# Value weights in quarters, half-depth value steps and another order in an attention and channel-mix kernel

## The chip, the cores and the metric

The kernel runs on one core of one Trainium2 chip. The metric is the device time of one execution in microseconds, lower is better.

## The reference

Eight batches of eight heads, 576 tokens, 64 dimensions each. Attention goes through 32 memory slots per head; its output, 512 wide, goes through a channel mix with squared relu and a sigmoid gate. All inputs are float32.

```python
a = softmax(phi, axis=2)                       # over the 576 tokens
k_m = einsum('bhsm,bhsd->bhmd', a, k)
v_m = einsum('bhsm,bhsd->bhmd', a, v)
attn = softmax(q @ k_m.T / 8)                  # over the 32 slots
x = (attn @ v_m)                               # 8 heads side by side: [8, 576, 512]
x_prev = x shifted by one token, zero first
xk = mu_k * x + (1 - mu_k) * x_prev
xr = mu_r * x + (1 - mu_r) * x_prev
k = relu(xk @ w_k)                             # 512 -> 1024
v = (k * k) @ w_v                              # 1024 -> 512
out = sigmoid(xr @ w_r) * v
```

## The kernel before, in words

Everything is issued in an order written out by hand: `PLAN` is a list of words, each names one step, and every engine gets its instructions in the order of the words. `BANKS` gives, one digit for each PSUM tile in the order in which tiles are asked for, which of the eight PSUM banks it takes. The order in which a step comes on one engine is therefore fixed; between engines semaphores decide.

The words: a number before the colon is a batch. `exp` exponentiates phi (ScalarE), `ko` makes the memory keys and the sums of the slots on TensorE, `v` the memory values (`kov` both), `zk` takes the reciprocals, `nk`/`ak` normalises keys on VectorE or ScalarE, `nv`/`av` the values, `tk`/`ta` transposes the keys and copies them out on VectorE or ScalarE, `q0`, `q1` transpose q on VectorE, `s` makes the scores and exponentiates them, `fe`, `fs`, `fo` (and `qe`, `qs`, `qo` in quarters) fold, sum and spread the denominators on VectorE, and `y0` to `y3` give the attention weights `atn` (L431). Batch 0 has its own way to the mixed input: `mk0`, `mk1`, `mr0`, `mr1` (L245 matmuls, then casts, L458) write the inputs of keys (k) and gates (r) for the first 320 and the last 256 tokens; each takes four PSUM banks. `busyNxM` issues N matmuls of zeros, M blocks of 128 columns wide (L215), which nothing reads.

From batch 1 on tokens go in chunks of 512 (the eighth 448), across batches. `x1:v` makes chunk 1's x in transposed form, ScalarE casting it (with `m` VectorE casts half), `d` subtracts the previous token, `k` and `r` scale the difference by mu and add it (scaled on VectorE with ending `d`, L562, on ScalarE with `e`, L560) into the rings `xkT` and `xrT`. Then follow

- `c1:3`: key matmuls for 128 of the 1024 features and a chunk's tokens (L617), relu on ScalarE (L621), square on VectorE (L629) or, with ending `s`, on ScalarE (L627). Chunk 0 is batch 0 and goes in halves, `a` of 320 and `b` of 256 tokens;
- `g:7`: the gate of a 128-token tile, four matmuls (L650) and a tanh (L653);
- `o:7`: the value of a tile, eight matmuls (L667), product with the gate on VectorE (L669), two stores. `o:1a` and `o:1b` are the halves of 256 columns.

There are 36 tiles for `g` and `o`. `p:` words are loads; almost all are issued on GpSimd's queue, in the order of the words, and cast float32 to bf16 on the way. `p:wk:4-8` is the half of wk for features 512 to 1023, `p:wv:0-2` the half of wv for output columns 0 to 255. Each buffer is loaded again only when its last reader is done.

Of the kernel before, what the change touches and what calls it, by code (L numbers as in the profile page):

```python
# [10 lines left out]
F32 = mybir.dt.float32  # L11
# [5 lines left out]


PLAN = [
# [24 lines left out]
]  # L44

LOADS = {None: ("phi", "k", "v", "q")}
PRE = "k:0a id:"
BANKS = (
    "01234567012367540123675403612754036127546203715462073154620731546207315462037416520374165724031567240315"
    "67203415672034162053472053416720534720516372401637254016354106732541067325410673254173254173065412730652"  # L50
    "73041652730416527304165274163052741630527416305276413052764130527641305276413"
)


NJ = 9
# [6 lines left out]
def kernel(  # L62
# [34 lines left out]
    psum = ctx.enter_context(tc.psum_pool(name="psum", bufs=1))  # L97
# [4 lines left out]
    def bank():  # L102
        return f"ps{next(banks)}"
# [16 lines left out]
    def load_phi(b, eng):  # L120
        ph = ld.tile([128, HH, NJ, M], F32, name="ph", tag=f"ph{b % 2}")
        eng.dma_start(out=ph.rearrange("p h j m -> p h (j m)"), in_=rows(phi[b]))
        loads[b] = ph

    def load_rows(dst, src):
        nc.gpsimd.dma_start(out=dst.rearrange("p h j d -> p h (j d)"), in_=rows(src))
# [25 lines left out]
    wv_sb = big.tile([128, NF, Dm], BF16, name="wv")  # L152
# [7 lines left out]
    def preload(word):  # L160

        what, _, part = word.partition(":")
        if what in weights:
            dst, src = weights[what]
            f0, f1 = (int(x) * 128 for x in part.split("-"))
            nc.gpsimd.dma_start(out=dst[:, :, f0:f1], in_=src[:, :, f0:f1])
        elif what == "id":
            make_identity(nc, identity)
        else:
            n = int(part[0])  # L170
            if what == "phi":
                load_phi(n, nc.gpsimd)
            else:
                dst = qs[n % 2].rearrange("p (h j) d -> p h j d", j=NJ) if what == "q" else kvs[:, KV[n % 2]["k1v".index(what)]]
                src = {"q": q, "k": k, "v": v}[what][n]
                if len(part) == 1:
                    load_rows(dst, src)
                elif part[1] in "ab":
# [20 lines left out]
    for g in range(4):  # L199
        r = slice(g * M, (g + 1) * M)  # L200
# [8 lines left out]
    sq = big.tile([128, NF, 2 * S], BF16, name="sq")  # L209
# [379 lines left out]
        return steps  # L589


    def store(o, t, cols):
        g = t * 128
        eng = nc.sync
        while g < (t + 1) * 128:
            b, r = divmod(g, S)
            p = g - t * 128
            j, p0 = divmod(r, QR)
            j = (j + 1) % NJ if b else j
            n = min(QR - p0, (t + 1) * 128 - g)  # L600
            dst = out[b].rearrange("(p j) d -> p j d", j=NJ)[p0:p0 + n, j, cols]
            eng.dma_start(out=dst, in_=o[p:p + n, cols])
            if t >= NTOK // 128 - 2:
                eng = nc.scalar
            g += n

    def keys(c):
        start = STARTS[c]
# [28 lines left out]
    gated, outs, homes, parts = {}, {}, {}, {}  # L637
    free = {"sg": list(range(SG)), "o": list(range(4))}

    def take(name, t):  # L640
        homes[name, t] = free[name].pop(0)
        return work.tile([128, Dm], F32, name=name, tag=f"{name}{homes[name, t]}")
# [10 lines left out]
            nc.scalar.activation(gated[t], pr, AF.Tanh, scale=0.5)  # L653
        return go

    def value(t, hs=((0, 1),), n=1):

        def go():
            if t not in outs:
                outs[t] = take("o", t)  # L660
            o = outs[t]
            p = t * 128 % (2 * S)
            for h0, h1 in hs:
                cols = slice(h0 * Dm // n, h1 * Dm // n)
                pv = psum.tile([128, Dm], F32, name="pv", tag=bank())
                for fi in range(NF):
                    nc.tensor.matmul(pv[:, cols], lhsT=sq[:, fi, p:p + 128],  # L667
                                     rhs=wv_sb[:, fi, cols], start=(fi == 0), stop=(fi == NF - 1))
                nc.vector.scalar_tensor_tensor(o[:, cols], in0=gated[t][:, cols], scalar=1.0, in1=pv[:, cols],  # L669
                                               op0=AL.add, op1=AL.mult)  # L670
                store(o, t, cols)
                parts[t] = parts.get(t, 0) + Dm * (h1 - h0) // n
            if parts[t] == Dm:
                for name in free:
                    free[name].append(homes[name, t])
        return go

    NT = NTOK // 128
    chunks = {f"x{c}": chunk_steps(c) for c in range(1, len(STARTS))}
    mixes = {f"c{c}": keys(c) for c in range(len(STARTS))}  # L680
    mixes["g"] = {str(t): gate(t) for t in range(NT)}
    mixes["o"] = {str(t): value(t) if t < NT - 1 else value(t, ((0, 1), (1, 2)), 2) for t in range(NT)}
    for t in range(4):
        for h in range(2):
            mixes["o"][f"{t}{'ab'[h]}"] = value(t, ((h, h + 1),), 2)

    attend = [attention(b) for b in range(B)]
    todo = []
    for n, word in enumerate(" ".join(PLAN).split()):
        who, _, name = word.partition(":")  # L690
# [40 lines left out]
```

## Time and profile before

| what | value |
|---|---|
| runs | 200.18, 202.08, 202.23 us, median 202.08 |
| profiled execution | 200.59 us, span 198.8 us |
| granted TensorE clock | 0.991 |
| busy: TensorE, VectorE, ScalarE, GpSimd | 189.0, 155.5, 149.7, 29.8 us |
| moved by the software queue of GpSimd | 20.91 MB |

Busy time of TensorE counts a matmul up to its modelled end, so that 95% doesn't say that no time can be saved; the places where it waits, and for what, tell more. Times of the trace count from the first instruction.

### The profile page before, as it was taken

The numbers are of one execution on the slowest core, as the hardware profiler recorded it, in microseconds if no ns is written. First come the engines' busy times: TensorE is split into PE (matmuls) and PEld (weight loads), VectorE is DVE, ScalarE is ACT, GpSimd is POOL, SyncE is SP. The second block draws the span as 40 slices with busy tenths as digits, with TensorE's granted clock in tenths as the row PEclk, the third lists the DMA queues.
The fourth block names the chain that finished last, engine by engine and source line by source line (L and its number), as shares of the span: only waits on it lengthen the run. The fifth ranks groups of instructions, "written<-read, shape, count | busy, mean of one in ns | idle before, by whom it ended". The sixth has DMA issues, their size and how long they took to land.

```text
span 198.8 us, 5486 instructions
## 1 busy us (share of the span) xinstructions
PE 189.0 (95%) x2194; PEld 97.4 (49%) x2214; DVE 155.5 (78%) x428; ACT 149.7 (75%) x307; POOL 29.8 (15%) x45
## 2 busy tenths in 40 slices
PE   8978799999999999999999999999999999999992
PEld 3535565784454544445347644444443445444451
DVE  6179589898879998999699999998999998122232
ACT  2245899748987999999998899997878698935210
POOL 7843323211050210003500000000000000000000
PEclk9979999999999999999999999999999999999999
DMA  6999999999999999994999903212142027004345
GB/s 160 183 206 268 206 208 199 267 224 276 250 224 279 232 302 218 266 299 64 207 208 248 227 2 83 53 31 53 44 108 63 1 47 167 0 3 106 81 97 139
DMA packets 24522, 31.30 MB, mean 157 GB/s; under 512 B 1960, under 2 KB 19632, under 8 KB 24496
## 3 DMA queue, kind: packets, MB, share of 16 engines
q0 software_dynamic: 17392, 20.91, 56.4%
q1 hardware_dynamic: 6336, 9.18, 17.9%
q10 hardware_dynamic: 768, 0.85, 1.4%
q8 instruction: 17, 0.28, 0.5%
q14 instruction: 9, 0.07, 0.1%
HBM read 38.28 MB, written 9.44 MB: 240 GB/s over the span
## 4 chain that ended last, share of the span: by engine, by line
PE 70%; DMA 13%; DVE 9%; ACT 3%; issue 1%; POOL 1%; POOLq 0%; DVEq 0%
PE pv L667 26%; PE pk L617 25%; PE pr L650 13%; DMA wr<-in_moe_w_r_dram 9%; DMA q<-in_q_dram 4%; PE kvps L279 3%; DVE o L669 1%; DVE diff L545 1%; DVE sq L629 1%; PE scps L371 1%; PE nops L245 1%; ACT x L536 1%; ACT sg L653 1%; DVE xrT L567 1%; DVE lz L422 1%
## 5 line engine op out<-in xcount | busy, mean ns | idle before, releaser
L617 PE MATMUL pk<-xkT,wk 128*128 128x512 bf16 (+4 forms) x344 | 67.3, 340 | 1.0 <-ACT xkT L458 0.3
L667 PE MATMUL pv<-wv,sq 128*128 128x512 bf16 (+1 forms) x324 | 65.3, 353 | 0.2
L621 ACT ACTIVATE rl<-pk 128x512 bf16<-128x512 f32 (+3 forms) x80 | 42.9, 555 | 6.8 <-PE pk L617 4.2
L617 PEld LDWEIGHTS <-wk 128*128 128x128 bf16 x352 | 32.9, 98 | 29.3 <-issue 1.5
L667 PEld LDWEIGHTS <-sq 128*128 128x128 bf16 x328 | 31.4, 98 | 29.5 <-issue 0.4
L650 PE MATMUL pr<-wr,xrT 128*128 128x512 bf16 x136 | 34.8, 380 | 0.6 <-DMA wr<-in_moe_w_r_dram 0.2
L669 DVE SCALAR_TENSOR_TENSOR o<-sg,pv 128x512 f32<-128x512 f32 (+1 forms) x41 | 24.4, 614 | 11.5 <-PE pv L667 11.4
L560 ACT ACTIVATE mu_d<-diff,mu 128x512 bf16<-128x512 bf16 (+1 forms) x40 | 26.2, 716 | 6.1 <-DVE diff L550 2.9
L653 ACT ACTIVATE sg<-pr 128x512 f32<-128x512 f32 x36 | 20.9, 601 | 9.4 <-PE pr L650 5.7
L629 DVE TENSOR_TENSOR sq<-rl 128x320 bf16<-128x320 bf16 (+5 forms) x63 | 17.6, 314 | 12.2 <-ACT rl L621 11.9
L627 ACT ACTIVATE sq<-rl 128x512 bf16<-128x512 bf16 (+5 forms) x41 | 21.7, 543 | 1.1
L650 PEld LDWEIGHTS <-xrT 128*128 128x128 bf16 x144 | 13.5, 98 | 16.5 <-issue 0.8
L536 ACT CAST x<-nops 128x512 bf16<-128x512 f32 (+3 forms) x34 | 16.0, 572 | 2.0 <-PE nops L245 2.0
L431 DVE TENSOR_TENSOR atn<-e,lz 128x320 bf16<-128x320 bf16 (+1 forms) x32 | 13.2, 442 | 0.2
L545 DVE TENSOR_TENSOR diff<-x 128x1024 bf16<-128x1024 bf16 (+1 forms) x15 | 10.5, 699 | 2.6 <-ACT x L536 2.6
L422 DVE STREAM_TRANSPOSE lz<-se 128x320 f32<-128x320 f32 (+3 forms) x22 | 12.3, 572 | 0.2
L376 ACT ACTIVATE e<-scps 128x288 bf16<-128x288 f32 x32 | 10.5, 421 | 2.4 <-PE scps L371 2.4
L265 ACT ACTIVATE em<-ph 128x1152 bf16<-128x1152 f32 (+1 forms) x9 | 9.3, 1053 | 3.5 <-DMA ph<-in_phi_dram 3.5
L356 DVE STREAM_TRANSPOSE qT<-q 128x576 uint32<-128x576 uint32 x16 | 11.9, 757 | 0.0
L215 PE MATMUL idle<-zeros 128*128 128x512 bf16 (+2 forms) x44 | 10.9, 414 | 1.0 <-DVE zeros L144 1.0
L413 DVE TENSOR_REDUCE se<-eT 128x18 f32<-128x576 bf16 (+3 forms) x16 | 11.1, 696 | 0.2
L279 PE MATMUL kvps<-kvs,em 64*32 64x64 bf16 (+2 forms) x864 | 10.0, 220 | 1.2 <-DMA kvs<-in_k_dram 1.2
(72 smaller groups left out, 148.1 us busy)
## 6 DMA issues: line engine op xcount, KB each, us to landing
out_dram<-o SPq DMA_DIRECT2D x61, 128.0 KB, 2.5
kvs<-in_v_dram POOLq DMA_DIRECT2D x8, 576.0 KB, 15.5
ph<-in_phi_dram POOLq DMA_DIRECT2D x7, 576.0 KB, 18.8
kvs<-in_k_dram POOLq DMA_DIRECT2D x7, 576.0 KB, 19.0
q<-in_q_dram POOLq DMA_DIRECT2D x6, 576.0 KB, 18.9
q<-in_q_dram POOLq DMA_DIRECT2D x4, 288.0 KB, 10.1
out_dram<-o SPq DMA_DIRECT2D x18, 64.0 KB, 5.6
wk<-in_moe_w_k_dram POOLq DMA_DIRECT2D x2, 512.0 KB, 14.3
```

Of the source, the lines that this page charges most:

```text
L279: nc.tensor.matmul(kvps[c][g * M:(g + 1) * M], lhsT=em[ROWS[c], j, g, :], rhs=kvs[ROWS[c], at, g, j, :], start=j == 0, stop=j == NJ - 1, s ...
L422: nc.vector.transpose(st["lz"].rearrange("p c (b t h) -> p (c b) h t", t=PB, h=2)[:, b0:b0 + n], st["se"][:, b0:b0 + n].unsqueeze(3).to_br ...
L536: (nc.vector.tensor_copy if both and i % 2 else nc.scalar.copy)(x[:, i, c0:c1], pss[i])
L560: nc.scalar.activation(t[:, i, :n], ds[c][:, pr + i, :n], AF.Copy, scale=mu1[:, o:o + 1])
L617: nc.tensor.matmul(pk[:, p0 - lo:p1 - lo], lhsT=wk_sb[:, di, fi * 128:(fi + 1) * 128], rhs=xk_T[:, di, p0 % RING:p0 % RING + p1 - p0], sta ...
L621: nc.scalar.activation(rl, pk, AF.Relu, scale=HALF_ROOT)
L627: nc.scalar.activation(sq[:, fi, p:p + p1 - p0], rl[:, part], AF.Square)
L629: nc.vector.tensor_mul(sq[:, fi, p:p + p1 - p0], rl[:, part], rl[:, part])
L650: nc.tensor.matmul(pr, lhsT=xr_T[:, di, c0:c0 + 128], rhs=wr_sb[:, di, :], start=(di == 0), stop=(di == ND - 1))
L653: nc.scalar.activation(gated[t], pr, AF.Tanh, scale=0.5)
L667: nc.tensor.matmul(pv[:, cols], lhsT=sq[:, fi, p:p + 128], rhs=wv_sb[:, fi, cols], start=(fi == 0), stop=(fi == NF - 1))
L669: nc.vector.scalar_tensor_tensor(o[:, cols], in0=gated[t][:, cols], scalar=1.0, in1=pv[:, cols], op0=AL.add, op1=AL.mult)
```

## The change

- wv comes in four loads: columns 0 to 255 and 256 to 511, each for features 0 to 511 (`l`) and 512 to 1023 (`u`).
- A value half of tiles 0 to 3 can be made in two steps of four matmuls, which share a PSUM bank: `e` and `f` for columns 0 to 255, `c` and `d` for 256 to 511. The bank stays taken from the first step of a tile until its last such step is evicted. In tile 1 all four steps share one bank, and only the first matmul of the first step carries the start flag.
- In the order: phi of batch 1 is loaded ahead of wk's first half; batch 0's four mixes stand together, and five of chunk 0's keys, from features 512 to 1023, stand ahead of batch 1's `ko`; all sixteen keys of chunk 0 stand ahead of the first gate; the other steps move by a few places, some change their engine.
- At the end tile 33 is made in halves, the second one last, and tile 35 whole. `store` is written anew; from tile 32 (before: 34) on the second of a tile's two stores is issued on ScalarE's queue.

```diff
 PLAN = [
-    "0:exp0 p:k:0b 0:busy3x3 0:busy21x4 0:mu 0:mub 0:exp1 0:k0c 0:k1c p:q:00 0:z 0:ha0 0:busy2x2 p:q:01 0:hn1 0:q0",
-    "0:q1 0:hc1 p:v:0 0:ht0 0:s1 0:fe1 0:fs1 0:s0 0:busy8x2 0:fo1 0:l1 0:l0 0:y2 0:v 0:nr0 0:h1z 0:busy4x2 p:wk:4-8",
-    "0:nr1 p:phi:1 0:h0z 0:y0 0:busy6x2 0:nk0 0:nk1 0:y1 0:y3 0:mk0 p:q:11 p:k:1 0:mk1 c0:5a 1:exp c0:4a c0:6as",
-    "c0:7bs 0:mr1 1:ko 1:zk0 1:zk1 p:wk:0-4 1:nk p:q:10 c0:4b 1:q1 c0:7a 1:ta 0:mr0 c0:0a 1:q0 c0:0b c0:3b c0:1a",
-    "c0:2a 1:s1 p:wr:0-4 p:v:1 1:s0 1:fe1 1:fs1 c0:2b c0:3as 1:qo2 1:qe1 g:2 1:qs1 g:0 p:wv:0-2 1:qo3 1:y2 g:3 1:qe0",
-    "g:1 1:qs0 1:qo0 1:y0 c0:1b 1:qo1 1:y3 1:y1 1:v 1:av c0:5bs c0:6b x1:v0m o:1a x1:v1 x1:d2d o:3a x1:d0d p:wv:2-4",
-    "x1:k2d o:2a x1:k0d o:3b o:0a p:phi:2 o:1b o:2b 2:exp p:k:2 x1:r2d o:0b x1:r0e 2:ko 2:zk1 p:q:2 c1:0s 2:zk0 2:nk",
...
-    "g:33 o:33 g:34 o:31 o:34 o:35",
+    "0:busy21x4 0:exp0 p:k:0b 0:exp1 0:busy1x4 0:z 0:k0c 0:k1c p:q:00 0:ha1 p:q:01 0:busy4x3 0:q0 0:ha0 0:mu 0:q1",
+    "p:v:0 0:ht0 0:mub 0:hc1 0:s1 0:s0 0:busy4x4 0:l0 0:fe1 0:h0z p:phi:1 0:l1 0:fs1 0:fo1 0:h1z 0:v 0:nk0 0:nk1 0:y3",
+    "0:y0 0:y2 1:exp 0:y1 0:nr1 0:busy5x3 p:wk:4-8 0:nr0 0:mk0 p:q:11 0:mk1 1:q1 0:mr1 0:mr0 c0:7a c0:4as c0:7b c0:4b",
+    "p:k:1 c0:5a 1:ko 1:zk0 p:wk:0-4 1:zk1 1:nk c0:6b c0:6a 1:tk c0:5b c0:3a p:q:10 c0:2b 1:q0 c0:3b c0:1a c0:0a",
+    "p:wr:0-4 1:s0 1:s1 c0:1bs 1:qe1 c0:2as c0:0bs g:1 1:fe1 p:v:1 p:wv:0-2l p:wv:0-2u 1:qs1 1:qe0 1:fs1 1:qs0 1:qo1",
+    "g:0 g:3 1:qo0 1:qo2 1:v 1:qo3 1:nv g:2 1:y1 o:3e p:wv:2-4l o:1e 1:y3 1:y2 1:y0 o:0e x1:v1m o:3f o:1f x1:v0 o:2e",
+    "x1:d0d x1:d2d o:1c x1:k0d p:wv:2-4u x1:k2e o:2b p:phi:2 x1:r0e o:0b 2:exp o:3b o:2f p:k:2 c1:5 c1:4 c1:3 2:ko",
...
+    "x8:r2d o:31 c8:7 g:28 c8:3s g:32 c8:6s o:28 o:30 g:35 g:33 o:29 o:32 o:33b g:34 o:35 o:34 o:33a",
 ]
@@ preload
-            f0, f1 = (int(x) * 128 for x in part.split("-"))
-            nc.gpsimd.dma_start(out=dst[:, :, f0:f1], in_=src[:, :, f0:f1])
+            f0, f1 = (int(x) * 128 for x in part.rstrip("lu").split("-"))
+            fis = {"l": slice(0, NF // 2), "u": slice(NF // 2, NF)}.get(part[-1], slice(0, None))
+            nc.gpsimd.dma_start(out=dst[:, fis, f0:f1], in_=src[:, fis, f0:f1])
@@ store
+        for n in range(2):
+            b, r = divmod(t * 128 + n * QR, S)
+            j = (r // QR + 1) % NJ if b else r // QR
+            eng = nc.scalar if n and t >= NTOK // 128 - 4 else nc.sync
+            eng.dma_start(out=out[b].rearrange("(p j) d -> p j d", j=NJ)[:, j, cols], in_=o[n * QR:(n + 1) * QR, cols])
@@ value
-    def value(t, hs=((0, 1),), n=1):
+    opened = {}
+
+    def value(t, hs=((0, 1),), n=1, f0=0, f1=NF):
...
-                pv = psum.tile([128, Dm], F32, name="pv", tag=bank())
-                for fi in range(NF):
-                    nc.tensor.matmul(pv[:, cols], lhsT=sq[:, fi, p:p + 128],
-                                     rhs=wv_sb[:, fi, cols], start=(fi == 0), stop=(fi == NF - 1))
+                pv = opened.get(t) if f1 - f0 < NF else None
+                fresh = pv is None
+                if fresh:
+                    pv = psum.tile([128, Dm], F32, name="pv", tag=bank())
+                if f1 - f0 < NF:
+                    opened[t] = pv
+                for fi in range(f0, f1):
+                    nc.tensor.matmul(pv[:, cols], lhsT=sq[:, fi, p:p + 128], rhs=wv_sb[:, fi, cols],
+                                     start=(fi == 0 and fresh), stop=(fi == NF - 1),
+                                     skip_group_check=f1 - f0 < NF)
+                if f1 < NF:
+                    continue
...
+            mixes["o"][f"{t}{'ec'[h]}"] = value(t, ((h, h + 1),), 2, 0, NF // 2)
+            mixes["o"][f"{t}{'fd'[h]}"] = value(t, ((h, h + 1),), 2, NF // 2, NF)
```

In the lines that are left out, squares on ScalarE (ending `s`) go from 35 to 32, scalings on VectorE (ending `d`) from 12 to 15 of 32, of chunk 1's eight squares ScalarE makes two for six, and chunk 7's x is cast by both engines. `BANKS` is written anew, with 283 digits for 285.

More of the change, by code (lines that the diff above doesn't have):

```diff
@@ L48 @@
 BANKS = (
-    "01234567012367540123675403612754036127546203715462073154620731546207315462037416520374165724031567240315"
-    "67203415672034162053472053416720534720516372401637254016354106732541067325410673254173254173065412730652"
-    "73041652730416527304165274163052741630527416305276413052764130527641305276413"
+    "01234567012435617024365174203651742035762143057621430756214307562143056720567120561205761205761324057613"
+    "24057613240512470563124705631247031245670143567012456370456312704563127045127630127630127630452630417630"
+    "147631047652310476523107456231074562301475623014756230147562301475623014756"
 )
@@ L592, in store @@
     def store(o, t, cols):
[L593 to L605, printed above, removed]
+        for n in range(2):
[3 more added lines that the diff above has]
+            eng.dma_start(out=out[b].rearrange("(p j) d -> p j d", j=NJ)[:, j, cols], in_=o[n * QR:(n + 1) * QR, cols])
     def keys(c):
@@ L654, in gate @@
         return go
-    def value(t, hs=((0, 1),), n=1):
+    opened = {}
+    def value(t, hs=((0, 1),), n=1, f0=0, f1=NF):
         def go():
-            if t not in outs:
-                outs[t] = take("o", t)
-            o = outs[t]
             p = t * 128 % (2 * S)
@@ L664, in go @@
                 cols = slice(h0 * Dm // n, h1 * Dm // n)
-                pv = psum.tile([128, Dm], F32, name="pv", tag=bank())
-                for fi in range(NF):
-                    nc.tensor.matmul(pv[:, cols], lhsT=sq[:, fi, p:p + 128],
-                                     rhs=wv_sb[:, fi, cols], start=(fi == 0), stop=(fi == NF - 1))
+                pv = opened.get(t) if f1 - f0 < NF else None
[10 more added lines that the diff above has]
+                    continue
+                if t not in outs:
+                    outs[t] = take("o", t)
+                o = outs[t]
                 nc.vector.scalar_tensor_tensor(o[:, cols], in0=gated[t][:, cols], scalar=1.0, in1=pv[:, cols],
@@ L672, in go @@
                 parts[t] = parts.get(t, 0) + Dm * (h1 - h0) // n
-            if parts[t] == Dm:
+            if parts.get(t) == Dm:
                 for name in free:
@@ L681 @@
     mixes["g"] = {str(t): gate(t) for t in range(NT)}
-    mixes["o"] = {str(t): value(t) if t < NT - 1 else value(t, ((0, 1), (1, 2)), 2) for t in range(NT)}
+    mixes["o"] = {str(t): value(t) for t in range(NT)}
+    for t in range(NT - 4, NT):
+        for name, h, n in (("a", (0, 1), 2), ("b", (1, 2), 2), ("i", (0, 3), 4), ("j", (3, 4), 4)):
+            mixes["o"][f"{t}{name}"] = value(t, (h,), n)
     for t in range(4):
@@ L685 @@
             mixes["o"][f"{t}{'ab'[h]}"] = value(t, ((h, h + 1),), 2)
+            mixes["o"][f"{t}{'ec'[h]}"] = value(t, ((h, h + 1),), 2, 0, NF // 2)
+            mixes["o"][f"{t}{'fd'[h]}"] = value(t, ((h, h + 1),), 2, NF // 2, NF)
+        mixes["o"][f"{t}l"] = value(t, f1=NF // 2)
+        mixes["o"][f"{t}u"] = value(t, f0=NF // 2)
     attend = [attention(b) for b in range(B)]
```

32 rows, old and new, of the table PLAN are left out of this document.

## The prediction

> **What bounds the kernel now.** I read the page first, then the busy times by stretch, then the engines' timelines up to 60 us and the DMA issues, and last the places where TensorE waited. The page's head, then the stretches (each engine's busy time and instruction count, then the granted clock, DMA share and GB/s):
>
> ```profile
> span 198.8 us, 5486 instructions
> PE 189.0 (95%) x2194; PEld 97.4 (49%) x2214; DVE 155.5 (78%) x428; ACT 149.7 (75%) x307; POOL 29.8 (15%) x45
> ```
> ```profile
> 0.00:30.00 30.00, 25.55 (x479) 14.72 (x480) 19.07 (x57) 16.16 (x41) 14.86 (x25) 0.94 1.11 205
> 30.00:45.00 15.00, 14.89 (x255) 10.64 (x258) 14.01 (x39) 10.61 (x23) 4.10 (x6) 1.00 1.28 230
> 45.00:95.00 50.00, 49.53 (x682) 23.70 (x687) 45.96 (x120) 46.61 (x96) 8.59 (x13) 1.00 1.07 241
> 95.00:120.00 25.00, 24.46 (x295) 13.71 (x302) 23.16 (x72) 23.04 (x45) 2.20 (x3) 1.00 0.89 172
> 120.00:165.00 45.00, 44.74 (x368) 20.15 (x349) 42.90 (x122) 38.35 (x78) 0.00 (x0) 1.00 0.25 57
> ```
>
> TensorE is full from 30 us on: it loses 0.11 us in 30 to 45, 0.47 in 45 to 95, 0.54 in 95 to 120. So an order can win there at most about one microsecond. What can still move is the stretch before 45 us, which runs at the pace of the loads, and the question whether VectorE (idle 1.8 us in 95 to 120, 2.1 in 120 to 165) still keeps up. The timeline of TensorE in the first stretch (start, length, then what; in brackets the idle time before):
>
> ```profile
> 17.50 1.36 PE L245 MATMUL mxps<-atn,vm 32*64 32x320 bf16 x40 [0.36 <-DVE vm L441]
> 19.12 2.32 PE L617 MATMUL pk<-xkT,wk 128*128 128x320 bf16 x16 [0.26 <-ACT xkT L458]
> ...
> 22.96 0.80 PE L279 MATMUL kvps<-kvs,em 64*32 64x128 bf16 x72 [1.16 <-DMA kvs<-in_k_dram]
> ...
> 25.55 2.68 PE L617 MATMUL pk<-xkT,wk 128*128 128x320 bf16 x20 [0.19 <-PE mxps L245]
> ...
> 29.97 3.63 PE L650 MATMUL pr<-wr,xrT 128*128 128x512 bf16 x15 [0.22 <-DMA wr<-in_moe_w_r_dram]
> ...
> 37.12 6.29 PE L667 MATMUL pv<-wv,sq 128*128 128x256 bf16 x56
> 43.34 0.80 PE L279 MATMUL kvps<-kvs,em 64*32 64x128 bf16 x72
> 44.07 3.63 PE L617 MATMUL pk<-xkT,wk 128*128 128x512 bf16 x15
> ```
>
> Prices from it: a 128x320 matmul 2.68/20 = 0.134 us, so a key of chunk 0's first half (four) 0.53; a 128x256 one 6.29/56 = 0.112, so a second-half key 0.45, a half of a value tile (eight) 0.9, and the new half-depth step (four) 0.45. Keys and slot sums of batch 2 (`ko`) take 44.07 - 43.34 = 0.73.
>
> The loads are one stream. wr as the chain of waits has it (start, length), then POOL's issues, then sizes and time to landing of batch 1's v and both wv issues:
>
> ```profile
> 11.52 18.41 DMA wr<-in_moe_w_r_dram
> ```
> ```profile
> 14.32 0.75 POOL L126 DMA_DIRECT2D kvs<-in_v_dram  x1 [2.05 <-DMA kvs<-in_v_dram]
> 17.08 0.88 POOL L166 DMA_DIRECT2D wv<-in_moe_w_v_dram  x1 [2.01 <-DMA wk<-in_moe_w_k_dram]
> 18.62 0.87 POOL L166 DMA_DIRECT2D wv<-in_moe_w_v_dram  x1 [0.65 <-DMA q<-in_q_dram]
> ```
> ```profile
> kvs<-in_v_dram POOLq DMA_DIRECT2D x1, 576.0 KB, 18.4
> wv<-in_moe_w_v_dram POOLq DMA_DIRECT2D x1, 512.0 KB, 18.4
> wv<-in_moe_w_v_dram POOLq DMA_DIRECT2D x1, 512.0 KB, 19.6
> ```
>
> Issue plus landing time: wr at 29.9, v of batch 1 at 32.7, wv's halves at 35.5 and 38.2; wk's second issue (columns 0 to 4) is there at 25.55 at the latest, when its first keys start. The stream delivers one block every 2.7 us, and TensorE's order must fit it.
>
> **The change, part by part.**
>
> *Loads.* The same bytes in nearly the same order; phi of batch 1 goes ahead of wk's first half, and v of batch 3 two blocks later (5.4 us), behind phi and k of batch 4; its use moves behind six more keys and two gates (eight groups of four 512-column matmuls, 3.63/15 x 32 = 7.7 us), so that costs nothing. wv comes in four quarters, so by halving the spacing they land at about 34.1, 35.5, 36.9 and 38.2. Two issues more on POOL, 2 x 0.88 us: POOL waits 2.0 and 0.65 us before these very issues, so they cost nothing unless the eight loads in flight no longer keep the engines fed (they hold fewer bytes now); then the next loads slip by up to 1.8 us. I take 0.
>
> The Trainium skill, "DMA: Bandwidth & Descriptors", section on the anatomy of one SWDGE DMA, gives about 2.0 us fixed cost per DMA. If that were paid serially, two more DMAs would put everything behind wv 4 us later. The trace speaks against it: 512 KB land every 2.7 us, and with 2 us of it fixed the rest would move at three times the 230 GB/s of the 30-to-45 row.
>
> *Keys of half of wk while k of batch 1 loads.* Before, the row at 22.96 waits 1.16 us for k with four keys done; batch 0's second r mix comes after it. In the new order both r mixes and five keys stand ahead of it. All four mixes in a row, of four PSUM banks each, go through the eight banks twice, so the r mixes must wait for the casts of the k mixes:
>
> ```profile
> 18.65 1.31 ACT L458 CAST xkT<-mxps 128x320 bf16<-128x320 f32 x4 [2.27 <-PE mxps L245]
> ```
>
> Four casts take 1.3 us per engine with the other four on VectorE beside them. With the first mix where it was (the row at 17.50; +-0.4 us, its inputs are reordered on VectorE), the r mixes end near 20.9 instead of the keys starting at 19.12. Bounds: 20.4 and 21.5. Then 7a, 4a, 7b, 4b, 5a = 3 x 0.53 + 2 x 0.45 = 2.5 us to 23.4, by when k (22.95) is there. 0.73 for its keys, 6b, 6a, 5b to 25.6, when wk's other half (25.55) is there, five more keys 2.5 us, scores 0.5, three last keys 1.43: 30.1 us, with wr at 29.9. So all sixteen keys are done when the gates can begin; before it was thirteen. Gain there 3 x 0.45 = 1.3 us; lower bound 0, if the mixes end at 21.5 and ScalarE (sixteen relus beside the casts) lags.
>
> *Value steps by quarters.* From 30.1: three gates 2.6 us, v of batch 1 from 32.8 to 33.6, gate 2 to 34.4, three half-depth steps 1.35 to 35.8 (first quarter there at 34.1), mixes 0.3, two second steps 0.9, mixes 0.3, two steps 0.9, then 2b, 0b, 3b and 2f, 3.15: 41.4 us. Before, the row at 37.12 ends the eight halves at 43.4. But chunk 1's keys, next in the order, need xkT, which VectorE makes from batch 1's weights (last of these, then xkT's last add):
>
> ```profile
> 35.69 0.72 DVE L431 TENSOR_TENSOR atn<-e,lz 128x256 bf16<-128x256 bf16 x2
> ...
> 42.27 0.69 DVE L567 TENSOR_TENSOR xkT<-x,mu_d 128x1024 bf16<-128x1024 bf16 x1
> ```
>
> Before this was ready at 42.96, 6.55 us after the weights, with TensorE there at 44.07. In the new order the weights end at the same time (scores follow the same q), one scaling goes to ScalarE (0.6 us) and one value eviction fewer stands between (0.4): 42.0. So TensorE waits 0.6 us. Steps 0f, 1d and batch 2's `ko` are still to come, 0.9 + 0.73. Equal work: 42.0 + 1.63 = 43.63 against 44.07. **-0.45 us** (from -1.3, if xkT is not late, to +0.8, if the mixes lag).
>
> *The other order, 45 to 165 us.* Work moves between ScalarE and VectorE. Their prices (mean ns of one):
>
> ```profile
> L629 DVE TENSOR_TENSOR sq<-rl 128x512 bf16<-128x512 bf16 x10 | 4.1, 421 | 7.5 <-ACT rl L621 7.5
> L562 DVE TENSOR_SCALAR mu_d<-diff,mu 128x512 bf16<-128x512 bf16 x20 | 6.4, 359 | 0.0
> L313 DVE TENSOR_SCALAR kbd<-kvps,rz 128x128 bf16<-128x128 f32 x9 | 2.8, 347 | 0.1
> L324 DVE TENSOR_SCALAR vb<-kvps,rz 128x64 bf16<-128x64 f32 x6 | 1.4, 278 | 0.3 <-PE kvps L279 0.3
> L536 DVE CAST x<-nops 128x320 bf16<-128x320 f32 x2 | 0.9, 480 | 0.0
> ```
>
> Over the kernel VectorE gets three squares (35 to 32 on ScalarE), three scalings (20 to 17) of two instructions, two wide casts of chunk 7, and gives up one kbd and one vb: 1.3 + 2.1 + 1.4 (the cast estimated from the 128x320 one by width, 0.7 each) - 0.7 - 0.55 = +3.5 us, ScalarE correspondingly less. Up to batch 6's weights, near 135 us, it is four squares, one scaling, less one kbd and one vb: 1.7 + 0.7 - 0.7 - 0.55 = +1.15 us. The hand-overs were tight:
>
> ```profile
> 56.27 1.19 DVE L431 TENSOR_TENSOR atn<-e,lz 128x256 bf16<-128x256 bf16 x3
> ```
> ```profile
> 57.68 0.42 PE L245 MATMUL nops<-atn,vb 32*64 32x512 bf16 x8
> ...
> 119.82 0.48 PE L371 MATMUL scps<-qT,kmT 32*32 32x288 bf16 x32 [0.38 <-ACT kmT L343]
> ```
>
> Weights ready at 57.46 for a use at 57.68, and a stall of 0.38 at 119.82. The four squares fall into 45 to 57, where VectorE has some of its 4.0 us idle in 45 to 95; what is left over costs between 0 and 1.15. I take **+0.2**, since that idle time is larger than what is added. Behind 165 us VectorE is idle most of the time and its surplus costs nothing. TensorE's own work is the same: ten halves of value tiles before and after (33 is halved now, 35 whole), and fillers of 131 blocks of 128 columns for 133, all ahead of the first mix, where TensorE waits anyway.
>
> *End.* The last eviction and what follows it:
>
> ```profile
> 195.01 0.42 DVE L669 SCALAR_TENSOR_TENSOR o<-sg,pv 128x256 f32<-128x256 f32 x1 [0.45 <-PE pv L667]
> ```
>
> A 256-column half stands last again (33a for the second half of 35), its two stores on SP and ScalarE's queue as before: 3.4 us, **0**.
>
> Sum: -0.45 + 0.2 = -0.25 us on the profiled execution's 200.59, 200.3. That execution lies 1.5 us under the runs' median: 200.18 and 200.59 form one level, 202.08 and 202.23 another. A median may fall on either (200.3 or 201.8); I give the middle, **201.0**. A measurement of this kernel tells about 1% from no change.
>
> **The rivals.**
> 1. *The new packing is kept whole (faster).* The 1.3 us of the keys stay because xkT is ready by 41.4, and ScalarE, relieved, no longer holds up TensorE, which gets back the 0.47 + 0.54 us that it loses from 45 to 120: -2.3, 198.3. For it: the row at 119.82 waits for ScalarE. Against it: xkT hangs on VectorE.
> 2. *VectorE becomes the bound (slower).* From 95 to 165 us 5 to 7% of its time are free. If its idle time earlier cannot be used because its inputs come late, the 1.15 us and chunk 7's casts, 1.4, push scores and mixes of batches 7 and 6 and then chunk 7's keys: +2.6 - 0.45, 202.7 on the profile's level, 204.2 on the upper. It decides once VectorE is idle under 1 us in 95 to 165, against 3.9 now. Against it: 4.0 us idle in 45 to 95.
> 3. *The start slips (slower).* The eight-bank wait, or fewer bytes in flight, put the gates or chunk 1 back: +0.8 + 1.8, 203.2, or 204.7 on the upper level. The half clock is part of it: the 0-to-30 row grants 0.94 where TensorE idles 4.5 us, and the new order has fewer fillers between 13 and 17 us. The Trainium skill, "TensorE: Matmul & The Clock Gate", part 1 on the HAM clock gate, puts an idle window of about 3.4 us before a half clock; the trace lost clock with gaps that were shorter.
> 4. *The quarters do nothing:* TensorE still waits for xkT at 42; that is inside my forecast.
>
> **How the numbers follow.** Forecast (within 1%, with 4) 0.42; rival 1 0.30; rival 2 0.16, rival 3 0.12. Its own range, from -1.3 to +0.8 + 1.15, is 199.3 to 202.5 on the profile's level. The range takes in rival 1 with the mixes at their early bound (-0.5 more, 197.8) and rivals 2 and 3 on the upper level: 197.8 to 204.7. Faster by over 1% 0.30, within 0.42, slower 0.28.
>
> **What would show it.** Right: no wait for k ahead of batch 1's kvps, sixteen pk groups before the first pr near 30 us, chunk 1's first pk at 41.5 to 42.5, VectorE about 159 us busy and ScalarE under 148, TensorE losing under 1.5 us between 45 and 165. Wrong: pr after 31 us, wv's last quarter after 39.5, or waits of TensorE on VectorE or on PSUM evictions that add to over 1.5 us.

## The result, and the profile after

The median of 20 runs is 199.81 us (199.28 to 201.53); the kernel before, run beside it, has 200.75 us over 20 runs (199.86 to 202.23). The ratio is 0.9947, 95% interval [0.9924, 0.9971]: half a per cent faster, and less than the 1% that the prediction set as its bound. The profiled execution takes 199.63 us, 0.96 less than the one before. Between sets of runs the kernel before has medians of 200.75 to 201.24, so each experiment below is compared with the kernel before of its own set.

The page's head and the busy times by stretch of the kernel after (columns as in the prediction):

```profile
span 197.9 us, 5488 instructions
PE 189.6 (96%) x2182; PEld 96.7 (49%) x2205; DVE 158.3 (80%) x440; ACT 146.9 (74%) x302; POOL 31.0 (16%) x47
```
```profile
0.00:30.00 30.00, 27.29 (x478) 15.09 (x479) 19.44 (x59) 16.82 (x41) 14.57 (x25) 0.94 1.11 206
...
45.00:95.00 50.00, 49.42 (x712) 23.74 (x721) 46.88 (x125) 45.26 (x94) 9.20 (x13) 1.00 1.03 225
95.00:120.00 25.00, 24.84 (x340) 14.30 (x343) 24.20 (x75) 22.20 (x47) 2.72 (x4) 1.00 1.00 204
120.00:165.00 45.00, 44.74 (x270) 19.84 (x274) 42.05 (x120) 36.29 (x75) 0.00 (x0) 1.00 0.32 72
```

TensorE is busy 1.74 us longer in the first 30 us (27.29 for 25.55) and 0.38 longer in 95 to 120. VectorE has 2.8 us more to do, ScalarE 2.8 less.

The start on TensorE's timeline:

```profile
17.31 3.18 PE L246 MATMUL mxps<-atn,vm 32*64 32x320 bf16 x80 [0.55 <-DVE atn L432]
20.42 2.68 PE L611 MATMUL pk<-xkT,wk 128*128 128x320 bf16 x20
23.27 0.80 PE L280 MATMUL kvps<-kvs,em 64*32 64x128 bf16 x72 [0.17 <-DVE sq L623]
...
25.88 2.68 PE L611 MATMUL pk<-xkT,wk 128*128 128x320 bf16 x20 [0.17 <-DMA wk<-in_moe_w_k_dram]
...
30.39 2.75 PE L644 MATMUL pr<-wr,xrT 128*128 128x512 bf16 x11
...
34.62 1.47 PE L665 MATMUL pv<-wv,sq 128*128 128x256 bf16 x12
...
41.48 2.76 PE L611 MATMUL pk<-xkT,wk 128*128 128x512 bf16 x11
44.17 0.80 PE L280 MATMUL kvps<-kvs,em 64*32 64x128 bf16 x72
44.91 1.90 PE L611 MATMUL pk<-xkT,wk 128*128 128x512 bf16 x7
```

The 1.16 us wait for k of batch 1 is gone, all sixteen keys of chunk 0 stand ahead of the first gate at 30.39, and from there to 45 the timeline marks no wait of TensorE. At 44.91 it has done three keys of chunk 1 that the kernel before had not done at 44.07 (12 matmuls, of which the row at 41.48 has 11 on record; some 2.6 us) and lacks steps 0f and 1d (0.9): 44.91 - 2.6 + 0.9 = 43.2, **0.9 us ahead**.

How the lead lives on, in four rows of TensorE's timeline (batch 2's mixes, batch 4's keys and values, batch 7's scores, batch 6's keys and values), and the same of before where the prediction does not show them:

```profile
56.80 0.42 PE L246 MATMUL nops<-atn,vb 32*64 32x512 bf16 x8
...
74.08 0.94 PE L280 MATMUL kvps<-kvs,em 64*32 64x192 bf16 x72
...
118.48 0.48 PE L372 MATMUL scps<-qT,kmT 32*32 32x288 bf16 x32
118.89 0.94 PE L280 MATMUL kvps<-kvs,em 64*32 64x192 bf16 x72
```
```profile
74.97 0.94 PE L279 MATMUL kvps<-kvs,em 64*32 64x192 bf16 x72
...
120.23 0.94 PE L279 MATMUL kvps<-kvs,em 64*32 64x192 bf16 x72
```

The lead is 0.88 at 57, 0.89 at 74 and 1.34 at 119; between the last two, the 0.38 us wait for ScalarE ahead of batch 7's scores has gone. The end gives some of it back. The last evictions and the landing of the last stores, after, then the landings before (KB each, us from issue to landing):

```profile
192.82 1.24 DVE L673 SCALAR_TENSOR_TENSOR o<-sg,pv 128x512 f32<-128x512 f32 x2 [1.10 <-PE pv L665]
```
```profile
out_dram<-o SPq DMA_DIRECT2D x2, 64.0 KB, 2.2
out_dram<-o ACTq DMA_DIRECT2D x2, 64.0 KB, 2.6
```
```profile
out_dram<-o SPq DMA_DIRECT2D x2, 64.0 KB, 2.0
out_dram<-o ACTq DMA_DIRECT2D x2, 64.0 KB, 2.2
```

The last eviction ends at 194.06, 1.37 us earlier than before (195.01 + 0.42 = 195.43). From there to the span's end are 3.84 us, before 3.37. So -1.37 + 0.47 = -0.9 us of span. I call that last stretch the tail.

### The profile page after: what moved, and what is told of

The parts are those of the page before. It is cut to its first block, busy times and chain, and to the rows that moved or that the text cites. A ratio compares the mean times of both kernels' runs of the same rounds, so it can differ in the third digit from the quotient of the medians.

```text
span 197.9 us, 5488 instructions
## 1 busy us (share of the span) xinstructions
PE 189.6 (96%) x2182; PEld 96.7 (49%) x2205; DVE 158.3 (80%) x440; ACT 146.9 (74%) x302; POOL 31.0 (16%) x47
## 4 chain that ended last, share of the span: by engine, by line
PE 82%; DMA 9%; POOL 4%; ACT 1%; issue 1%; DVE 1%; POOLq 0%
PE pk L611 30%; PE pv L665 30%; PE pr L644 16%; DMA wk<-in_moe_w_k_dram 9%; PE kvps L280 4%; PE nops L246 2%; PE scps L372 1%; POOL q L183 1%; POOL kvs L126 1%; ACT x L537 1%; ACT mu_d L561 1%; POOL kvs L129 1%; POOL ph L122 0%; POOL wk L167 0%; DVE diff L546 0%
## 5 line engine op out<-in xcount | busy, mean ns | idle before, releaser
L647 ACT ACTIVATE sg<-pr 128x512 f32<-128x512 f32 x36 | 20.9, 601 | 9.7 <-PE pr L644 9.5
L561 ACT ACTIVATE mu_d<-diff,mu 128x512 bf16<-128x512 bf16 x34 | 22.4, 717 | 3.6 <-DVE diff L551 2.1
L623 DVE TENSOR_TENSOR sq<-rl 128x192 bf16<-128x192 bf16 (+5 forms) x66 | 18.9, 319 | 7.7 <-ACT rl L615 7.0
L621 ACT ACTIVATE sq<-rl 128x512 bf16<-128x512 bf16 (+5 forms) x38 | 19.8, 535 | 1.0
L537 ACT CAST x<-nops 128x512 bf16<-128x512 f32 (+3 forms) x32 | 15.1, 560 | 4.0 <-PE nops L246 4.0
L432 DVE TENSOR_TENSOR atn<-e,lz 128x256 bf16<-128x256 bf16 (+1 forms) x32 | 13.0, 445 | 0.1
L423 DVE STREAM_TRANSPOSE lz<-se 128x256 f32<-128x256 f32 (+2 forms) x24 | 12.0, 527 | 0.1
L216 PE MATMUL idle<-zeros 128*128 128x512 bf16 (+1 forms) x35 | 10.7, 466 | 1.0 <-DVE zeros L144 1.0
L414 DVE TENSOR_REDUCE se<-eT 128x18 f32<-128x576 bf16 (+3 forms) x17 | 11.2, 659 | 0.2
L568 DVE TENSOR_TENSOR xrT<-x,mu_d 128x1024 bf16<-128x1024 bf16 (+3 forms) x18 | 10.9, 613 | 0.5 <-ACT mu_d L561 0.2
```

Of the source, the lines that this page charges most:

```text
L423: nc.vector.transpose(st["lz"].rearrange("p c (b t h) -> p (c b) h t", t=PB, h=2)[:, b0:b0 + n], st["se"][:, b0:b0 + n].unsqueeze(3).to_br ...
L432: nc.vector.tensor_mul(st["at"][:, c, sl], st["e"][:, c, sl], st["lz"][:, c, sl])
L537: (nc.vector.tensor_copy if both and i % 2 else nc.scalar.copy)(x[:, i, c0:c1], pss[i])
L561: nc.scalar.activation(t[:, i, :n], ds[c][:, pr + i, :n], AF.Copy, scale=mu1[:, o:o + 1])
L621: nc.scalar.activation(sq[:, fi, p:p + p1 - p0], rl[:, part], AF.Square)
L623: nc.vector.tensor_mul(sq[:, fi, p:p + p1 - p0], rl[:, part], rl[:, part])
```

## The experiments

**The start alone, the rest alone.** The first has the order of after up to batch 2's `ko` and from there the order and the end of before; the second the reverse.

```diff
# start alone: after, then from "2:ko" on as before
-"2:ko 2:zk0 p:q:2 2:zk1 x1:r2d 2:q1 2:q0 2:ak c1:0 c1:2 2:ta c1:1 o:0f o:1d 2:s ..."
+"2:ko o:0f o:1d 2:zk1 p:q:2 c1:0s 2:zk0 x1:r2d 2:nk c1:1s 2:q1 c1:7s 2:tk p:v:2 g:6 2:q0 c1:2 2:s ..."
# rest alone: before, then from "2:ko" on as after
-"2:ko 2:zk1 p:q:2 c1:0s 2:zk0 2:nk c1:3 c1:1s 2:q1 c1:7s 2:tk p:v:2 g:6 2:q0 c1:2 2:s ..."
+"2:ko 2:zk0 p:q:2 2:zk1 c1:5 c1:4 c1:3 2:q1 2:q0 2:ak c1:0 c1:2 2:ta c1:1 2:s ..."
```

> The new order up to batch 2's keys, then the old order with its old end. Theory (the gain is made at the start, TensorE is 0.8 us ahead at equal work once batch 2's keys are done): -0.8 us against before, TensorE's last value matmul at about 194.2, and the wait of 0.4 us before the scores of batch 7 comes again, near 119. Rival (the gain is made by the order behind 45 us, the start's lead is eaten by VectorE): within 0.2 us of before.

> The old order up to batch 2's keys, then the new order with the new end. Theory (start): -0.1 to -0.4 us against before, which is the wait before batch 7's scores that does not come, less what the end loses; TensorE's last matmul at about 194.4. Rival (rest): -0.8 us or more, last matmul at 193.7.

Measured: 201.45 us for the start alone, ratio 1.0004 [0.9975, 1.0033]; 201.29 for the rest alone, 0.9999 [0.9976, 1.0022], beside 201.24 for the kernel before. Neither half gains by its time; for the first that is what the rival said. In its profile `ko` starts at 44.00 with three keys of chunk 1 done and steps 0f and 1d to come, so the lead is there, and then the mixes of batch 2 wait:

```profile
44.00 0.80 PE L280 MATMUL kvps<-kvs,em 64*32 64x128 bf16 x72
...
50.15 0.47 PE L372 MATMUL scps<-qT,kmT 32*32 32x288 bf16 x32
...
57.59 0.81 PE L246 MATMUL nops<-atn,vb 32*64 32x512 bf16 x8 [0.90 <-DVE atn L432]
```

From scores to weights VectorE needs 7.5 to 8 us (before 49.47 to 57.46, after 48.59 to 56.06). The order of before puts the scores of batch 2 behind the same number of steps however many keys are done already: they come at 50.15, later than before, and the mixes start at 57.59, before 57.68. The order of after puts the scores ahead of the remaining keys, at 48.59. So the keys done early become time only with the new order behind them. The 0.38 us wait for ScalarE ahead of batch 7's scores (at 120.06) is there again in this run too. The second half's rows:

```profile
57.93 0.42 PE L246 MATMUL nops<-atn,vb 32*64 32x512 bf16 x8
...
75.22 0.94 PE L280 MATMUL kvps<-kvs,em 64*32 64x192 bf16 x72
...
120.01 0.94 PE L280 MATMUL kvps<-kvs,em 64*32 64x192 bf16 x72
```

It is 0.25 us behind the kernel before at 58 and 75 and 0.22 ahead at 120: 0.47 gained between, without the start. The 0.25 is not a late start: its `ko` of batch 2 comes at 43.37, level with 43.34 before, and 0.2 us of it appear just behind that, where chunk 1's keys start at 44.28 for 44.07, for which the profile names no releaser. Its new end takes that back, with a tail of 3.77.

**The new order up to batch 2's mixes, then the old.** Two tries, since the first laid a value tile where its eviction was late (TensorE waited 0.48 at 58.30 for an eviction and 1.41 at 66.00 for batch 3's queries).

```diff
# after up to "x2:v", then as before
-"x2:v p:k:3 3:ko 3:zk p:q:3 x2:d0d x2:d2d 3:nk 3:q1 x2:k0e p:phi:4 3:q0 x2:k2e o:6 o:7 3:ta o:5 x2:r0e 3:s ..."
+"x2:v p:k:3 o:6 3:ko 3:zk x2:d0d p:q:3 3:q1 x2:d2d 3:ak o:7 x2:k0e 3:q0 p:v:3 x2:k2e o:5 3:ta x2:r2d 3:s ..."
# second try
+"x2:v p:k:3 3:ko 3:zk x2:d0d p:q:3 3:q1 x2:d2d 3:ak o:6 o:7 x2:k0e 3:q0 p:v:3 x2:k2e o:5 3:ta x2:r2d 3:s ..."
```

> The new order up to chunk 2's x (near 57 us), then the old order with its old end. In the first hybrid the start's lead of 0.8 us was lost at chunk 2's x, where TensorE waited 0.9 us for VectorE's weights of batch 2. Theory (the order between 45 and 57 us is the other half: it makes those weights earlier): no wait there, TensorE 0.8 us ahead of before from there to batch 7's scores, whose wait of 0.4 us comes again; -0.7 to -0.9 us against before. Rival (the lead is lost at the next weights of the old order just as well): a wait at chunk 3's or 4's x, within 0.3 us of before.

> The kernel after up to and including batch 2's values and mixes (x2:v), and from there the order and the end of the kernel before, with value tile 6 put ahead of tile 7 and behind batch 3's key weights, so that no eviction is late at the seam. Theory (the lead of the start is kept only if batch 2's weights come in the new order too; the order behind x2:v adds the 0.4 us at batch 7's scores, the old end saves 0.45 us of tail): x2:v at 56.7 to 57.0 against 57.7 before, the 0.38 us wait on ScalarE at batch 7's scores still there, tail 3.4 us, 199.7 to 200.2 beside 200.6 for the kernel before, ratio 0.995 to 0.998. Rival (the lead is eaten by VectorE wherever the old order follows): the lead at batch 3's or 4's weights is under 0.3 us, ratio 0.999 to 1.003.

Measured: 202.77, ratio 1.0105 [1.0067, 1.0143], and 201.43, 0.9994 [0.9968, 1.0020]. The second, at batch 3:

```profile
57.52 0.42 PE L246 MATMUL nops<-atn,vb 32*64 32x512 bf16 x8
...
64.08 0.28 PE L339 MATMUL ktps<-identity,kbd 128*128 128x128 bf16 x2
64.82 0.49 PE L372 MATMUL scps<-qT,kmT 32*32 32x288 bf16 x32 [0.46 <-ACT kmT L344]
```

Its start is 0.73 us later than that of the kernel after (first gate at 31.12 for 30.39), so its mixes are 0.16 ahead of the kernel before in the profile, and would be 0.9 ahead at an equal start. From mixes to scores it takes 7.30 us, the kernel before 6.53 (57.68 to 64.21). There a value tile stands between the transposition of the keys (`ktps`) and the scores and covers the copy on ScalarE; here that tile is already done, and the trip of 0.74 us lies bare. The rival named a loss at batch 3, and the lead is lost there, but to this seam and not to VectorE's weights. Both runs leave open what an order that is old behind 57 us but has no seam would take.

**The copy of batch 7's keys.**

```diff
# before
-"... o:16 g:19 g:18 7:ta o:17 ..."
+"... o:16 g:19 g:18 7:tk o:17 ..."
```

> The kernel before with one edit: the copy of batch 7's transposed keys (kmT) on VectorE instead of ScalarE, as the kernel after has it. Theory: the 0.38 us wait ahead of batch 7's scores at 119.8 is ScalarE's queue order and goes away, 0.3 us less, ratio 0.998 to 0.999. Rival: VectorE is as late there, the wait stays and is named DVE, ratio 1.000 to 1.002.

Measured: 202.10, ratio 1.0066 [1.0029, 1.0103]: worse. ScalarE's queue before and after, then VectorE's and TensorE's in this run:

```profile
118.45 1.06 ACT L653 ACTIVATE sg<-pr 128x512 f32<-128x512 f32 x2
119.40 0.37 ACT L343 COPY kmT<-ktps 128x256 bf16<-128x256 bf16 x1
```
```profile
117.24 0.52 ACT L323 ACTIVATE vb<-kvps,rz 128x64 bf16<-128x64 f32 x2
117.63 0.39 ACT L344 COPY kmT<-ktps 128x256 bf16<-128x256 bf16 x1
```
```profile
120.49 0.68 DVE L669 SCALAR_TENSOR_TENSOR o<-sg,pv 128x512 f32<-128x512 f32 x1
121.09 0.28 DVE L343 COPY kmT<-ktps 128x256 bf16<-128x256 bf16 x1
...
121.43 0.48 PE L371 MATMUL scps<-qT,kmT 32*32 32x288 bf16 x32 [1.35 <-DVE kmT L343]
```

Before, the copy stands behind two sigmoids. VectorE is even further behind: the wait grows from 0.38 to 1.35 us. (The transposed keys come 0.64 us later than before in this profile, 118.08 for 117.44; that is a late start, and the other 0.97 is the wait.) The wait's absence in the kernel after is therefore no change of engine, for the copy stays on ScalarE. By the rows it is the queue: two short scalings of values (0.52 us) instead of two sigmoids (1.06) stand just ahead of the copy, which ends 0.46 us before its use. No run moved the sigmoids alone. The expectation says that the kernel after has the copy on VectorE; its row shows ScalarE.

**wv in halves again, and the quarters in the wrong order.**

```diff
# a: in halves
-"p:wv:0-2l p:wv:0-2u ... p:wv:2-4l ... p:wv:2-4u"
+"p:wv:0-2 ... p:wv:2-4"
# b: first two quarters swapped
-"p:wv:0-2l p:wv:0-2u"
+"p:wv:0-2u p:wv:0-2l"
```

> The changed kernel with wv in two column halves again (at the places of the first quarter of each). Theory (the quarters let the three first half-depth steps run before 35.5 us, and xkT comes just in time): TensorE waits about 0.8 us before the first value step near 34.7, chunk 1's x and its keys come that much later, +0.6 to +0.8 us against the changed kernel. Rival (the split hides nothing, because chunk 1's keys wait for VectorE anyway): the wait is there but chunk 1's keys start at the same 41.7, +0.0 to +0.2 us.

> The changed kernel with the first two quarters of wv in the other order, so that the one which the first three half-depth steps read lands at 35.5 instead of 34.1 us; as many loads and instructions. Theory (quarters matter): TensorE waits 0.7 to 0.9 us before the first value step, chunk 1's keys start that much later than 41.7, +0.6 to +0.9 us against the changed kernel. Rival (chunk 1's x waits for batch 1's weights anyway): chunk 1's keys at 41.7 to 42.0, +0.0 to +0.3.

Measured: 201.08, ratio 0.9983 [0.9954, 1.0012], and 200.98, 0.9988 [0.9963, 1.0013]. First step of the values in halves, the landing of its first load, and the same step with the quarters swapped:

```profile
35.85 1.47 PE L665 MATMUL pv<-wv,sq 128*128 128x256 bf16 x12
```
```profile
17.43 0.88 POOL L167 DMA_DIRECT2D wv<-in_moe_w_v_dram  x1 [2.00 <-DMA ph<-in_phi_dram]
```
```profile
wv<-in_moe_w_v_dram POOLq DMA_DIRECT2D x1, 512.0 KB, 18.4
```
```profile
35.83 1.47 PE L666 MATMUL pv<-wv,sq 128*128 128x256 bf16 x12 [0.75 <-ACT sg L648]
```

The whole half lands at 17.43 + 18.4 = 35.8, and the values start at 35.85. There is no wait in that profile only because its start was 1.2 us late (1.95 us without work at 15 to 17 us, for which it shows no releaser). With the quarters swapped the first gate was 0.3 late and TensorE waits 0.75 us; the profile names a sigmoid, but the quarter, issued at 19.59 with 16.2 us to landing, is there at 35.8. In the kernel after the values start at 34.62. Chunk 1's keys then start at 42.69 for 41.48. So the right quarter at the right time is worth about 0.9 us at the start (1.21 less the 0.3). For the halves the landing at 35.8 says the same, but their profile, late by itself, shows no wait. By the medians next to nothing is left of the change in either run; the intervals still overlap a little with that of the kernel after, [0.9924, 0.9971].

**The wait for k put back.**

```diff
-"0:mr1 0:mr0 c0:7a c0:4as c0:7b c0:4b p:k:1 c0:5a 1:ko"
+"0:mr1 0:mr0 p:k:1 1:ko c0:7a c0:4as c0:7b c0:4b c0:5a"
```

> The changed kernel with batch 1's keys and sums ahead of the five early keys of chunk 0. Theory (the early keys fill the wait for k): TensorE waits about 2.4 us for k from 20.5 to 22.95; the first gate comes near 32.4 instead of 30.4 and chunk 1's keys about 1.5 to 2 us later; +1.5 to +2.0 us against the changed kernel. Rival (wr, v and wv, which land where they land, pace the start, and early keys only move the waiting): the gates come later, but chunk 1's keys within 0.5 us, +0.0 to +0.5.

Measured: 204.85, ratio 1.0196 [1.0159, 1.0233], and 4.2 us more than the kernel after by the profiled executions (203.83 for 199.63), where the theory had 1.5 to 2.0. The row of TensorE, and two stretches with the granted clock (third number from the end):

```profile
23.27 1.16 PE L281 MATMUL kvps<-kvs,em 64*32 64x128 bf16 x72 [2.13 <-DMA kvs<-in_k_dram]
```
```profile
22.00:23.00 1.00, 0.00 (x0) 0.00 (x0) 0.73 (x2) 0.00 (x0) 0.00 (x0) 0.83 1.24 208
23.00:26.00 3.00, 2.73 (x79) 1.82 (x80) 0.00 (x0) 0.35 (x1) 0.74 (x1) 0.50 1.22 205
```

The wait is 2.13 us, and the clock falls to half within it: 0.83 in the stretch from 22 to 23 puts the fall near 22.66, 1.5 us into the wait, and 0.96 from 26 to 27 puts its end near 26.08. `ko` starts at 23.27 as in the kernel after, but the gates at 34.59 for 30.39 and chunk 1's keys at 45.69 for 41.48, so the rival is refuted. Of these 4.2 us the five keys, now behind `ko`, are some 2.5, and half of the work from 23.27 to 26.08 is 1.4, the price of the half clock (both are estimates from the rows). In these profiles, then, the five early keys do more than fill a wait: with them the clock stays at 1.00 there.

**Three more squares on VectorE in chunk 5** (1.3 us), to see how near it is to being the bound.

```diff
-"c5:6s ... c5:5s ... c5:1s"
+"c5:6 ... c5:5 ... c5:1"
```

> The changed kernel with three squares of chunk 5 (keys 6, 5 and 1) moved from ScalarE to VectorE, 1.3 us more for VectorE between 108 and 125 us. Theory (VectorE is within 0.2 to 0.9 us of setting the pace there, as the prediction's second rival has it): TensorE waits at batch 6's scores or at chunk 6's x, +0.4 to +1.1 us against the changed kernel. Rival (VectorE has room): no new wait over 0.2 us, same time.

Measured: 201.08, ratio 0.9994 [0.9967, 1.0022].

```profile
127.11 0.28 PE L340 MATMUL ktps<-identity,kbd 128*128 128x128 bf16 x2 [0.88 <-ACT kbd L313]
...
129.92 0.48 PE L373 MATMUL scps<-qT,kmT 32*32 32x288 bf16 x32
```

Batch 7's scores come 0.25 us later than in the kernel after (118.73), batch 6's 1.29 (128.63 there): 1.04 of 1.3 us reach TensorE. The wait stands ahead of the transposition of batch 6's keys and is named after ScalarE's `kbd`; ScalarE in turn needs VectorE's reciprocals, the last of which comes 1.29 us later as well (126.54 for 125.25), behind the three squares. VectorE has some 0.3 us to spare here.

**The end.** Three kernels: the old end in full; the old order of the last tiles with the new choice of queue; the old end with tile 35 cut at three quarters of its columns.

```diff
# a: old end
-"o:33b g:34 o:35 o:34 o:33a"            eng = nc.scalar if n and t >= NTOK // 128 - 4
+"o:33 g:34 o:34 o:35a o:35b"            eng = nc.scalar if n and t >= NTOK // 128 - 2
# b: the order alone       + "o:33 g:34 o:34 o:35a o:35b", and - 4 as in after
# c: a, and                + "o:35i o:35j"
```

> The changed kernel with the old end: tile 33 whole, tile 35 last and in halves, second stores on ScalarE's queue from tile 34 on only. Theory (the 0.5 us that the end took longer in the changed kernel's profile, 3.85 against 3.37 us behind the last eviction, is scatter of the last stores' landing): within 0.2 us of the changed kernel. Rival (the new end costs them): -0.4 to -0.5 us against the changed kernel, and 3.4 us behind the last eviction.

> The kernel after with the order of its last value tiles as before (33 whole, tile 35 in two halves last), while from tile 32 on the second store still goes out on ScalarE's queue. It parts the two edits of the end. If the order is the cause of the longer tail (a small last store behind tile 34's two 128 KB stores): tail back to 3.4 us and 0.4 us faster than the kernel after. If the queue is (more stores of the last tiles on ScalarE's queue): tail stays at 3.8 us, same time as after.

> The kernel after with the end of before (33 whole, second stores on ScalarE's queue only for the last two tiles) and the last tile cut into three quarters and one quarter of its columns instead of halves. Theory: the last eviction reads 128 columns instead of 256 and the last matmuls are half as long, so the span ends about 0.2 us earlier than with halves, tail 3.2 us, 199.2 to 199.6, ratio 0.991 to 0.995. Rival: the larger part's store (96 KB a half) is still moving when the last one starts, tail 3.4 us or more, no gain over halves.

Measured: 199.88 us, ratio 0.9940 [0.9917, 0.9963]; 199.72, 0.9924 [0.9901, 0.9946]; 199.99, 0.9938 [0.9911, 0.9965]. The last eviction of b, then that of c and c's issues on ScalarE's queue (count, duration in ns, first and last start):

```profile
193.93 0.42 DVE L674 SCALAR_TENSOR_TENSOR o<-sg,pv 128x256 f32<-128x256 f32 x1 [0.45 <-PE pv L666]
```
```profile
193.51 0.75 DVE L674 SCALAR_TENSOR_TENSOR o<-sg,pv 128x384 f32<-128x384 f32 x2 [0.56 <-PE pv L666]
```
```profile
L600 ACTq DMA_DIRECT2D out_dram<-o x3: 499/553/781, 193.0 to 194.7; - x3
```

With the old order alone the tail is 197.7 - 194.35 = 3.35 us, with the old end in full 3.42 (its last eviction ends at 194.58, the span at 198.0); all six kernels with the new order of the last tiles have 3.73 to 3.84. So the longer tail needs the new order; with the old order the choice of queue makes no difference. The new order with the old choice of queue was not run. In the order of after the last half tile's stores are issued right behind the 128 KB stores of tile 34 and land in 2.2 and 2.6 us; with another half tile between they land in 2.0 and 2.1 (b). The cut at three quarters does bring the last eviction to 194.26, but the last stores are issued only at 194.7: the two evictions end 0.2 us apart, and an issue holds its queue for 0.55. Its tail is 3.84, and nothing is gained.

b's start is 0.27 us late (chunk 1's keys at 41.75 for 41.48), so its span of 197.7 is 0.4 to 0.5 us less than that of the kernel after at an equal start. As a time that isn't shown: the intervals of all these kernels and of the kernel after overlap. By the profiles b is the best version, the new start and order with the old order of the last tiles.

## Why the prediction was right in part

The forecast was a change within 1%, 0.25 us less on the profile; it is within 1%, and 0.96 less on the profile, 0.5% in the medians. The sum had the right sign, but each of its three terms was off: the start's gain was put too small by 0.45 us, the order behind 45 us was taken for a cost and was a gain (0.65 apart), and a loss of 0.47 at the end was put at nothing. That the last works against the other two is luck. So is the agreement in relative terms, half a per cent: 201.0 lies half a per cent under 202.08, the median of three runs, because it is the middle of two levels (200.3 and 201.8), and the measured 199.81 lies half a per cent under a median of twenty runs, 200.75. The upper level did not come; 199.81 is below the lower one.

**The start, -0.45 forecast, -0.9 found.** The r mixes end at 20.5 (forecast 20.9, early bound 20.4); five keys stand ahead of `ko`, which waits 0.17 us (forecast none); sixteen keys are done before the first gate at 30.39 (30.1). The quarters' issues on POOL (first and last start) and their time to landing, longest for the first and shortest for the last:

```profile
L167 POOL DMA_DIRECT2D wv<-in_moe_w_v_dram x4: 740/740/742, 16.8 to 23.5; - x4
...
DMA to landing us min/median/max: 14.4/16.0/17.2
```

They land from 34.0 to 37.9, 1.3 us apart; the forecast had 34.1 to 38.2. The Trainium skill, "DMA: Bandwidth & Descriptors", anatomy of one SWDGE DMA, gives a fixed cost of about 2.0 us per DMA. The prediction weighed whether loads in a row pay it one after the other; here they don't, since four loads 1.3 us apart leave no room for it.

What was mis-sized is the wait for xkT, 0.6 us, which did not come. xkT's last adds:

```profile
40.34 1.53 DVE L568 TENSOR_TENSOR xkT<-x,mu_d 128x1024 bf16<-128x1024 bf16 x2
```

The row ends at 41.87, close to the forecast 42.0, but chunk 1's keys start at 41.48 without a wait. It holds two adds, each for 1024 of xkT's 2048 columns, and by the kernel's code a key's four matmuls go through the features in order: the first two need only the first add. The prediction took the last add as the condition of the first matmul. Without that 0.6 the term would have been -1.05. The rival "the new packing is kept whole" has no wait for xkT either, though by another reason (xkT whole at 41.4), and its start (-1.3 by its own count) is about as far from the 0.9 found as the forecast is.

A reading of the prediction was loose as well: a row's count can lack a record (x15 for 16 matmuls, x11 for 12), so that 3.63/15 is too much for one matmul, while its 2.6 us for three gates is about right (30.39 to 33.07).

**The order behind 45 us, +0.2 forecast, -0.45 found.** Both signs of this term stood in the prediction: as a cost here and as 1.0 us of gain in the first rival. VectorE's 158.3 us (forecast 159) and ScalarE's 146.9 (under 148) are right, and so is that VectorE hides its surplus: idle in 95 to 165 are 70 - 24.20 - 42.05 = 3.75 us, before 3.94. But the 0.38 us stall at 119.82 was counted as if it stayed; in the new order it went, and in the run with the old order behind the new start it stayed. TensorE loses 0.58 us in 45 to 95, about as before (0.47), and 0.16 for 0.54 in 95 to 120; up to 165 it loses 1.0 us, under the 1.5 that the prediction gave as a sign of being right.

**The end, 0 forecast, +0.47 found.** "A 256-column half stands last again" was true and not enough: it matters what is issued just ahead of its stores.

**The rivals.** VectorE as the bound did not come, but the mechanism is real: 1.3 us more in chunk 5 cost 1.04. The point from which it decides was set at under 1 us of idle time in 95 to 165; in chunk 5 it was reached although VectorE was still idle for 70 - 24.24 - 42.06 = 3.70 us there in that run, so idle time summed over 70 us was the wrong measure: what counts is the slack at one hand-over. The start's slip (eight banks, half clock) did not come in the kernel after, and its half clock came in the experiment with the wait put back. That the quarters do nothing is refuted: swapped, they cost about 0.9 us at the start.

## What to carry to other kernels

A lead won in one stage is time only if the next hand-over to a slower engine is moved up with it; look at where the following scores or weights start, not at how much work is done. When a wait for a transfer is costed, ask which part of a tile the first instruction reads, and split the load that the first reader waits for. At the end of a kernel, keep the last small stores apart from large ones issued just before.

## What the runs showed of the hardware

The granted clock fell to 0.50 for some 3.4 us (22.66 to 26.08) 1.5 us into a wait of TensorE of 2.13 us. A wait of 1.16 us in the kernel before and one of 1.66 us in the run with the copy of batch 7's keys moved left it at 1.00; the rows of the latter:

```profile
23.90 0.80 PE L279 MATMUL kvps<-kvs,em 64*32 64x128 bf16 x72 [1.66 <-DMA kvs<-in_k_dram]
```
```profile
23.00:26.00 3.00, 2.10 (x95) 1.64 (x102) 1.36 (x7) 1.82 (x7) 0.74 (x1) 1.00 1.22 206
```

The Trainium skill, "TensorE: Matmul & The Clock Gate", part 1 on the HAM clock gate, puts an idle window of about 3.4 us before a half clock. Here it came after less idle time in one piece, so a wait need not be that long to cost clock. The length of the wait alone isn't shown to be the cause either: 3.2 us of small mixes stand ahead of it here, and mostly keys in the other two runs. And the kernel before itself has the half clock early on, where the longest wait of TensorE in the 3 us ahead of it is 0.44 us:

```profile
13.00:14.00 1.00, 1.00 (x6) 0.70 (x5) 0.60 (x2) 0.94 (x4) 0.00 (x0) 0.50 1.25 214
```

What decides stays open.

64 KB stores land in 2.0 to 2.2 us, and in 2.2 to 2.6 right behind 128 KB stores on the same queues.

From run to run the first loads land at different times: v of batch 0 lands 9.5 to 11.2 us from its issue, and wr at 29.7 in the kernel after and at 30.5 in the second try with the old order from batch 3 on, whose first gate is 0.73 us later as well. Differences under 0.5 us are therefore read from the profiles at an equal start.
